# Attention state in 64-column chunks, the third token tile on the ACT queue, and a key fold interleaved with MLP units

## The chip, the cores and the metric

One core of one Trainium2 chip runs the whole kernel. The metric is the device time in microseconds of one execution (us), where lower is better. Engines are named as in the profile: PE multiplies matrices (PEld is its loading of weights, the stationary operand), DVE is the vector engine, ACT the scalar engine, POOL the general one, and SP only issues DMAs here.

## The reference

The input x has 2048 tokens of 640 features. It is normalised, and two branches read the normalised tokens: a linear attention with 32 heads of 20 columns, and a gated MLP with 1536 hidden columns. Their sum and x make the output.

```python
def _A_ref(x, wqkv, w_phi, wo):                      # S = 2048, D = 640, H = 32, Dh = 20
    q, k, v = split(x @ wqkv)                        # by head
    pq, pk = q @ w_phi, k @ w_phi                    # per head, 20x20
    phi_q = concat([softmax(pq), softmax(-pq)])      # 40 features per head
    phi_k = concat([softmax(pk), softmax(-pk)])
    kv, z = phi_k.T @ v, sum_s(phi_k)                # the state: 40 x 20 and 40 per head
    o = (phi_q @ kv) / (phi_q @ z + 1e-6)
    return merge_heads(o) @ wo
def _B_ref(x, w1, w3, w2):
    return (silu(x @ w1) * (x @ w3)) @ w2
xn = _layernorm(x)
out = x + _A_ref(xn, A_wqkv, A_w_phi, A_wo) + _B_ref(xn, B_w1, B_w3, B_w2)
```

## The kernel before

**How the work is tiled.** Tokens come in 16 tiles of 128, in `x_tok`, and in four blocks of 512 for the MLP. Features come in five chunks of 128. `xnT` holds the normalised tokens with features on partitions. Tiles 0 to 3 are transposed by PE (`xn_transpose`) and copied out of PSUM by ACT or DVE; the others by transposing DMAs on SP's queue. `w_phi` is folded into the key and query weights ahead of use: `fold_mm(1, dc)` makes chunk `dc` of `Wkp` with six small matmuls from `wqkT` (the key weights, loaded transposed by a DMA) and `BDc` (a block-diagonal `w_phi` made by POOL), and copies it out of PSUM. Values go to `v2` in 21 columns per head, of which the last is 1.0, so that the sum z comes with the same matmul.

**The attention state.** Key features lie in `ekt`. `kv_sum(half, k)` multiplies them with `v2` in 11 chunks of three heads (120 feature rows, 63 columns; the last chunk has two heads and 42 columns), each summed over the 16 token tiles. DVE multiplies the result with the mask `FM`, which keeps each head's own block, and writes it to `KVc`, a bf16 tile of 11 chunks of 63 columns that lie without a gap. `q_tok(t, k)` then takes one token tile: 11 matmuls with the transposed query features `EqT` as the stationary operand and one chunk of `KVc` as the moving operand, then a reciprocal and a product on DVE. `EqT` is written by a transposing DMA per token tile, from `eqt`, on SP's queue.

**What sets the order.** The program is written as twelve generator streams (`norms`, `transposes`, `fold_k`, `attention`, `mlps`, `outs` and others), each of which yields its next step or waits for a count in `done`. A planner holds a cost for every operation, takes at each step the stream whose head could start first by these costs, and appends its operations to the fixed instruction list of each engine. So an edit of one step can move others that it doesn't name. At run time each engine executes its list in order and waits on semaphores. All instructions are made by two helpers, so the profile names two lines: L102 (`op`) for computing and L114 (`dma`) for transfers.

**The opening.** `first_loads` (line 412) issues the first transfers. SP's queue has, in this order: token tile 0, chunks 0 and 1 of the value weights `wv`, token tile 2, chunks 2 and 3 of `wv`, chunk 4 of `wv`, token tile 3, a third of `w1` and of `w3` for the MLP, `w_phi`, the transposed key weights `wqkT`, and more tokens and weights. ACT's queue has token tile 1 alone. Each tile then goes through statistics (`ln_sums`, `ln_rstd`), `ln_apply` on DVE, `xn_transpose` on PE, copies to `xnT`, and the value matmuls `v_half` in two halves `q` of five matmuls each, which `v_out` copies to `v2`. `evac` gives a copy to ACT or DVE, whichever the planner believes free first. An MLP unit (`mlp(b, fc, k)`) has ten matmuls of 512 columns, one ACT operation and two on DVE; it needs all four tiles of its block.

**The key fold.** The stream `fold_k` (line 732) yields the five steps of `fold_mm(1, dc)` one after the other, with nothing that holds them apart:

```python
def fold_k():
    for dc in range(DC):
        yield lambda dc=dc: fold_mm(1, dc, banks(2))
    done["f"] += 1
```

The count `done["m"]` is that of the MLP units placed so far. `attention` goes on to the key features only once `done["f"]` is 1.

Of the kernel before, what the change touches and what calls it, by code (L numbers as in the profile page):

```python
# [3 lines left out]
ACT = mybir.ActivationFunctionType  # L4
ALU = mybir.AluOpType
# [5 lines left out]
H = 32  # L11
DH = 20
# [5 lines left out]
QC = 11  # L18
EPS = 1e-5
DEN_EPS = 1e-6  # L20
# [5 lines left out]
def heads_of_chunk(c):  # L26
    return (128 * c) // DH, (128 * c + 127) // DH
# [216 lines left out]
def bass_parallel_sum__linear_kernel_hedgehog__glu_gated_swiglu__prompt_kernel(  # L244
# [11 lines left out]
    bf = DT.bfloat16  # L256
# [6 lines left out]
    P = _Program(nc)  # L263
# [6 lines left out]
    def region(size):  # L270
        o = top[0]
        top[0] = o + (size + 31) // 32 * 32
        assert top[0] <= arena_size, top[0]
        return a0 + o

    def new(name, shape, dtype, offset=None):
        size = mybir.dt.size(dtype)
        for n in shape[1:]:
            size *= n
        return P.sbuf(name, shape, dtype, region(size) if offset is None else offset)  # L280
# [12 lines left out]
    FM = new("FM", [128, 6, 3], bf)  # L293
# [13 lines left out]
    x_tok = new("x_tok", [128, T, D], bf, RX)  # L307
# [22 lines left out]

    RW = region(13696)
    wqkT = new("wqkT", [128, 2 * DC, D], bf, RW)
    KVc = new("KVc", [128, QC, 63], bf, RW)
    eqt = new("eqt", [128, 3, QC * 128], bf, RW + 1408)
    o_tok = new("o_tok", [128, 3, D], bf, RW + 9856)
    EqT = [EqT0, EqT1]
# [5 lines left out]
    def bank(k, cols=512, off=0, rows=128):  # L342
        return PS[0:rows, k * 512 + off:k * 512 + off + cols]

    def bank2(k, cols):
        return PS[:, k * 512:(k + 2) * 512].rearrange("p (b c) -> p b c", c=512)[:, :, 0:cols]


    def mm(o, l, r, start, stop, shared=False, cost=None):
        n = free(r)  # L350
        P.op("PE", "matmul", [o], [l, r], (o, l, r),
             dict(start=start, stop=stop, skip_group_check=shared),
             cost=max(n / 2400 + 0.003, 0.055) if cost is None else cost)
# [5 lines left out]
    def free(ap):  # L359
        n = 1  # L360
        for s in ap.shape[1:]:
            n *= s
        return n
# [5 lines left out]
    def tt(eng, o, a, b, f, fast=1):  # L369
        c = 0.16 + free(o) / 960 / fast if eng == "DVE" else 0.2 + free(o) * 1.7 / 1000  # L370
        P.op(eng, "tensor_tensor", [o], [a, b], (o, a, b, f), cost=c)

    def stt(o, a, s, b, f0, f1):
        P.op("DVE", "scalar_tensor_tensor", [o], [a, b], (),
             dict(out=o, in0=a, scalar=s, in1=b, op0=f0, op1=f1), cost=0.16 + free(o) / 960)
# [7 lines left out]
    def evac(o, i):  # L383

        a = P.free["ACT"] + 0.17 + free(o) / 1200
        d = P.free["DVE"] + 0.14 + free(o) / 960 / (2 if i.dtype == bf else 1)
        copy("ACT" if a <= d else "DVE", o, i, 2 if i.dtype == bf else 1)
# [10 lines left out]
    x_t = A_x.rearrange("b (t p) d -> p (b t) d", p=128)  # L398
# [6 lines left out]
    def w13(a, b):  # L405
        P.dma("SP", w1_s[:, :, a:b], w1_t[:, :, a:b])
        P.dma("SP", w3_s[:, :, a:b], w3_t[:, :, a:b])

    def load_x(a, b):
        P.dma("SP", x_tok[:, a:b, :], x_t[:, a:b, :])  # L410

    def first_loads():
        load_x(0, 1)
        o = P.dma("ACT", x_tok[:, 1:2, :], x_t[:, 1:2, :])
        o.reads = P.regions(zero[:])
        for a, b in ((0, 2), (2, 4), (4, DC)):
            P.dma("SP", wv[:, a:b, :], wqkv_t[:, a:b, 2 * D:3 * D])
            if a != 2:
                load_x(2 + a // 4, 3 + a // 4)
        w13(0, 512)  # L420
        P.dma("SP", phi_s[:], phi_t)
        P.dma("SP", wqkT[:, DC:2 * DC, :], A_wqkv[:, D:2 * D], True)
        load_x(4, 8)
        load_x(8, 12)
        w13(512, 1024)
# [94 lines left out]
    def fold_mm(which, dc, k):  # L520
        first = [True, True]
        for e in range(DC):
            h0, h1 = heads_of_chunk(e)
            lo, hi = DH * h0, DH * (h1 + 1)
            for q in range(2):
                a, b = max(lo, 320 * q), min(hi, 320 * q + 320)
                if a < b:
                    mm(bank(k + q, b - a, a - 320 * q), wqkT[:, which * DC + e, 128 * dc:128 * dc + 128],
                       BDc[:, e, a - lo:b - lo], first[q], e == DC - 1 or (q == 0 and e == 2), True)
                    first[q] = False  # L530
        dst = (Wqp, Wkp)[which]
        evac(dst[:, dc, :].rearrange("p (b c) -> p b c", c=320), bank2(k, 320))
# [78 lines left out]
    def kv_sum(half, k):  # L611
        c0, c1 = ((0, 6), (6, QC))[half]
        for c in range(c0, c1):
            n = min(63, H * 21 - 63 * c)
            for t in range(T):
                m = min(128, (T - t) * 1280 - 120 * c)
                f = ekt[:].rearrange("p t f -> p (t f)")[:, 1280 * t + 120 * c:1280 * t + 120 * c + m]
                mm(bank(k, n, 63 * (c - c0))[0:m, :], f, v2[:, t, 63 * c:63 * c + n],
                   t == 0, t == T - 1, True, 0.03)
        n = min(6 * 63, H * 21 - 63 * c0)  # L620
        o = KVc[:, c0:c1, :].rearrange("p c (g d) -> p (c g) d", d=21)[:, 0:n // 21, :]
        i = bank(k, n).rearrange("p (g d) -> p g d", d=21)
        m = FM[:].rearrange("p c g -> p (c g)")[:, 0:n // 21]
        tt("DVE", o[:, :, 0:DH], i[:, :, 0:DH], m.unsqueeze(2).to_broadcast([128, n // 21, DH]), ALU.mult)
        stt(o[:, :, DH], i[:, :, DH], DEN_EPS / 2, m, ALU.add, ALU.mult)

    def q_tok(t, k):
        b, j = divmod(t, 4)
# [53 lines left out]
    def banks(n):  # L682

        def free_at(k):
            return max([o.end for i in range(k, k + n) for o in P.bank.get(("P", i), {}).values()],
                       default=0.0)
        return min(range(0, 8, n), key=free_at)

    done = dict.fromkeys(("w", "ln", "t", "f", "k", "v", "n", "kv", "p", "pn", "pt", "q", "o", "h", "m", "first"), 0)

    landed, pace, force = {}, [0], [False]

    def norms():
        yield lambda: (memset("DVE", zero[:], 0.0), memset("DVE", warm[:], 0.0), first_loads(), consts())
        yield lambda: act_sums(1)
        yield lambda: ln_stats(0, 1)
# [34 lines left out]

    def fold_k():
        for dc in range(DC):
            yield lambda dc=dc: fold_mm(1, dc, banks(2))
        done["f"] += 1

    done["w"] = 8
# [65 lines left out]
    def attention():  # L803
# [29 lines left out]
        while done["n"] < T:  # L833
            yield None
        yield lambda: kv_sum(0, banks(1))
        yield lambda: kv_sum(1, banks(1))
        done["kv"] = 1
        yield lambda: P.dma("SP", w2_s[:], B_w2.rearrange("(c p) d -> p c d", p=128))
# [23 lines left out]
    def outs():  # L862
        for t in range(T):
            while done["o"] <= t or done["h"] <= t // 4:
                yield None
            yield lambda t=t: out_tile(t, banks(2))

    streams = [norms(), transposes(), fold_k(), attention(), k_norms(), loads(), queries(), q_norms(),
               q_transposes(), o_transposes(), mlps(), outs()]
    MLPS, ATTN = 10, 3  # L870
    URGENT = {0: 4.0, 4: 4.0, 7: 4.0, 8: 4.0, 9: 4.0}
    n = len(streams)
    heads, alive = [None] * n, [True] * n
    while any(alive):
        best = None
        for i in range(n):
# [14 lines left out]
            if any(o.eng == "PE" for o in ops):  # L891
                at = max(P.ready(ops), P.free["PE"] + 0.15)
# [4 lines left out]
            else:  # L897
                at = P.start_of(ops[0])
                if i in URGENT:
                    now, mine = P.free["PE"], P.free[ops[0].eng]  # L900
                    if at <= max(now, mine) + 0.3 and at < now + URGENT[i]:
                        at = now + 0.1 - URGENT[i]
# [5 lines left out]
        i, ops, after = best[2:]  # L908
# [65 lines left out]
```

## Time and profile before

| | |
|---|---|
| median of 8 runs | 268.83 us (268.71 to 269.04) |
| the profiled execution's own time | 268.68 us |
| its span in the profile | 267.0 us |
| PE busy | 262.4 us, 98% of the span, 1951 matmuls |
| DVE, ACT, POOL busy | 182.8, 105.3, 96.2 us |
| granted PE clock | 1.00 |
| DMA traffic | 27.73 MB, mean 104 GB/s |

The span is what the profile covers; 1.7 us of the execution's time lie around it. Matmuls are pipelined: one of 63 columns is shown with 193 ns, but a new one can start every 30 ns or so. What a matmul costs the engine is therefore the distance between two starts, which the timeline gives as the distance of two groups divided by their count, and not its mean duration. A group named after its first shape can hold others: the ten matmuls of 63 columns and the one of 42 of a `q_tok` are shown as one group of eleven.

### The profile page before, as it was taken

To read this page: it belongs to the slowest core of one execution; us is meant where nothing else is said; L and a number is where in the kernel's file an instruction comes from. 1 tells how busy PE (TensorE), PEld (TensorE's weight loads), DVE (VectorE), ACT (ScalarE), POOL (GpSimd) and SP (SyncE) were. 2 spreads that over 40 slices of the span, in tenths; PEclk is the share of its full clock that TensorE was granted. 3 is DMA by queue.
4 is the path that set the end of the run, shared out by engine and by line. 5 is a ranking of instruction groups with operands and counts; after the bars stand their busy time and mean duration, and the time that the engine had idled before them with its cause. 6 is when DMAs were issued, how large, how long until landed. Compare 5 with 4: busy or idle time off the path is not lost.

```text
span 267.0 us, 4817 instructions
## 1 busy us (share of the span) xinstructions
PE 262.4 (98%) x1951; PEld 162.6 (61%) x1951; DVE 182.8 (68%) x315; ACT 105.3 (39%) x224; POOL 96.2 (36%) x107
## 2 busy tenths in 40 slices
PE   7999999999999999999999999999999999999996
PEld 2655666777645846567556565647455656777773
DVE  4669897998756697998697477758587955412112
ACT  5457978988565025440422404322244310000000
POOL 4313475799995163335233030340303330000000
PEclk9999999999999999999999999999999999999999
DMA  7993799620000198364643504260613035431211
GB/s 224 290 320 108 119 264 234 116 109 2 0 0 0 11 341 162 61 121 94 140 85 69 127 29 79 49 139 22 128 27 80 0 70 114 98 101 49 77 49 49
DMA packets 62742, 27.73 MB, mean 104 GB/s; under 512 B 49920, under 2 KB 62720, under 8 KB 62720
## 3 DMA queue, kind: packets, MB, share of 16 engines
q1 hardware_dynamic: 62576, 27.26, 42.8%
q8 instruction: 15, 0.25, 0.4%
q10 hardware_dynamic: 144, 0.16, 0.2%
q14 instruction: 7, 0.06, 0.1%
HBM read 12.81 MB, written 2.62 MB: 58 GB/s over the span
## 4 chain that ended last, share of the span: by engine, by line
PE 97%; DMA 1%; DVE 1%; ACT 0%; POOL 0%; issue 0%
PE PS L102 97%; DMA x_tok<-in_A_x_dram 1%; DVE bst L102 0%; ACT xnT L102 0%; POOL rstd L102 0%; DVE x_tok L102 0%; DVE xnT L102 0%; DVE xres L102 0%; DVE mv L102 0%
## 5 line engine op out<-in xcount | busy, mean ns | idle before, releaser
L102 PE MATMUL PS<-xnT,w_s 128*128 128x512 bf16 x480 | 107.7, 379 | 0.0
L102 PEld LDWEIGHTS PS<-xnT,w_s 128*128 128x128 bf16 x480 | 46.6, 98 | 52.1 <-ACT Wkp L102 0.2
L102 POOL TENSOR_TENSOR eqt<-eqt,rS 128x600 bf16<-128x600 bf16 (+1 forms) x32 | 41.1, 1307 | 92.5 <-DVE rS L102 92.5
L102 ACT ACTIVATE th<-PS 128x512 f32<-128x512 f32 x48 | 28.5, 597 | 80.8 <-PE PS L102 80.7
L102 PE MATMUL PS<-w_s,hT 128*128 128x320 bf16 (+2 forms) x384 | 54.9, 299 | 0.0
L102 DVE SCALAR_TENSOR_TENSOR t<-th,PS 128x512 bf16<-128x512 f32 x48 | 32.3, 673 | 27.3 <-ACT th L102 27.2
L102 PEld LDWEIGHTS PS<-w_s,hT 128*128 128x128 bf16 x384 | 37.1, 98 | 15.1
L102 POOL TENSOR_TENSOR ekt<-ekt,rS 128x640 bf16<-128x640 bf16 x32 | 39.5, 1274 | 6.7 <-DVE rS L102 6.7
L102 DVE TENSOR_TENSOR xres<-PS,xres 128x640 bf16<-128x640 f32 (+2 forms) x17 | 13.4, 786 | 37.7 <-PE PS L102 37.7
L102 ACT ACTIVATE eqt<-PS 128x240 bf16<-128x240 f32 (+1 forms) x96 | 27.1, 348 | 21.9 <-PE PS L102 17.9
L102 DVE SCALAR_TENSOR_TENSOR hT<-t,PS 128x512 bf16<-128x512 bf16 x48 | 33.0, 687 | 1.7
L102 DVE TENSOR_REDUCE S<-eqt 128x66 f32<-128x1320 bf16 x16 | 24.3, 1518 | 3.1 <-ACT eqt L102 3.1
L102 PE MATMUL PS<-wv,xnT 128*128 128x320 bf16 x160 | 24.5, 299 | 0.5 <-DVE xnT L102 0.2
L102 ACT ACTIVATE ekt<-PS 128x640 bf16<-128x640 f32 x32 | 22.4, 704 | 6.5 <-PE PS L102 5.9
L102 PE MATMUL PS<-wo_s,oT 128*128 128x320 bf16 (+2 forms) x160 | 24.5, 299 | 0.0
L102 PE MATMUL PS<-Wqp,xnT 128*128 128x360 bf16 (+1 forms) x160 | 24.2, 299 | 0.0
L102 PE MATMUL PS<-Wkp,xnT 128*128 128x320 bf16 x160 | 24.0, 299 | 0.0
L102 DVE TENSOR_REDUCE S<-ekt 128x64 f32<-128x1280 bf16 x16 | 23.0, 1437 | 0.0
L102 DVE RECIPROCAL rS<-S 128x64 f32<-128x64 f32 (+1 forms) x32 | 17.9, 560 | 3.3 <-POOL ekt L102 2.2
L102 PEld LDWEIGHTS PS<-Wqp,xnT 128*128 128x128 bf16 x160 | 15.2, 98 | 7.4
L102 PEld LDWEIGHTS PS<-wv,xnT 128*128 128x128 bf16 x160 | 15.3, 98 | 7.0 <-ACT xnT L102 0.7
L102 PEld LDWEIGHTS PS<-Wkp,xnT 128*128 128x128 bf16 x160 | 15.5, 98 | 6.2
(52 smaller groups left out, 152.8 us busy)
## 6 DMA issues: line engine op xcount, KB each, us to landing
w_s<-in_B_w_dram SPq DMA_DIRECT2D x6, 640.0 KB, 7.6
xres<-in_A_x_dram SPq DMA_DIRECT2D x16, 160.0 KB, 2.5
out_dram<-xres SPq DMA_DIRECT2D x15, 160.0 KB, 1.9
x_tok<-in_A_x_dram SPq DMA_DIRECT2D x3, 640.0 KB, 5.1
w_s<-in_B_w_dram SPq DMA_DIRECT2D x1, 1920.0 KB, 8.0
wo_s<-in_A_wo_dram SPq DMA_DIRECT2D x1, 800.0 KB, 4.7
wv<-in_A_wqkv_dram SPq DMA_DIRECT2D x2, 320.0 KB, 4.0
x_tok<-in_A_x_dram SPq DMA_DIRECT2D x3, 160.0 KB, 4.2
```

Source lines behind the costliest of these rows:

```text
L102: o = _Op(eng, lambda: m(*args, **kw), r, w, cost)
```

## The change

It has three parts. First, a chunk of `KVc` gets 64 columns in place of 63, with the last one unused, so that chunks begin 128 bytes apart; since heads are no longer evenly spaced over the whole tile, the masking in `kv_sum` works on four-dimensional views, and the second half, which ends with the chunk of two heads, is masked in two passes. Second, token tile 2 is issued by ACT's queue behind token tile 1, and SP's queue issues the three parts of `wv` one after the other and then token tile 3. Third, `fold_k` remembers the count of MLP units after its first step, and doesn't offer its third step before one more MLP unit is placed, and its fifth before two more are.

```diff
-    KVc = new("KVc", [128, QC, 63], bf, RW)
+    KVc = new("KVc", [128, QC, 64], bf, RW)
...
         o = P.dma("ACT", x_tok[:, 1:2, :], x_t[:, 1:2, :])
         o.reads = P.regions(zero[:])
+        P.dma("ACT", x_tok[:, 2:3, :], x_t[:, 2:3, :])
         for a, b in ((0, 2), (2, 4), (4, DC)):
             P.dma("SP", wv[:, a:b, :], wqkv_t[:, a:b, 2 * D:3 * D])
-            if a != 2:
-                load_x(2 + a // 4, 3 + a // 4)
+        load_x(3, 4)
...
-        n = min(6 * 63, H * 21 - 63 * c0)
-        o = KVc[:, c0:c1, :].rearrange("p c (g d) -> p (c g) d", d=21)[:, 0:n // 21, :]
-        i = bank(k, n).rearrange("p (g d) -> p g d", d=21)
-        m = FM[:].rearrange("p c g -> p (c g)")[:, 0:n // 21]
-        tt("DVE", o[:, :, 0:DH], i[:, :, 0:DH], m.unsqueeze(2).to_broadcast([128, n // 21, DH]), ALU.mult)
-        stt(o[:, :, DH], i[:, :, DH], DEN_EPS / 2, m, ALU.add, ALU.mult)
+        w = c1 - c0 - half
+        for a, b, g in ((0, w, 3), (w, c1 - c0, 2))[0:1 + half]:
+            o = KVc[:, c0 + a:c0 + b, 0:21 * g].rearrange("p c (g d) -> p c g d", d=21)
+            i = bank(k, 21 * g * (b - a), 63 * a).rearrange("p (c g d) -> p c g d", g=g, d=21)
+            m = FM[:, a:b, 0:g]
+            tt("DVE", o[:, :, :, 0:DH], i[:, :, :, 0:DH], m.unsqueeze(3).to_broadcast([128, b - a, g, DH]), ALU.mult)
+            stt(o[:, :, :, DH], i[:, :, :, DH], DEN_EPS / 2, m, ALU.add, ALU.mult)
...
     def fold_k():
         for dc in range(DC):
+            while dc and dc % 2 == 0 and done["m"] < at + dc // 2:
+                yield None
             yield lambda dc=dc: fold_mm(1, dc, banks(2))
+            if dc == 0:
+                at = done["m"]
         done["f"] += 1
```

In the instruction lists that come out, PE has the same 1951 matmuls in another order, from the third token tile on. The first difference, with the matmuls counted by shape:

```
before                                     after
 wv of tiles 0 and 1        320 x16         wv of tiles 0 and 1        320 x16
 transposes of tile 2       128 x5          transposes of tile 2       128 x5
 wv of tile 2, first half   320 x5          wv of tile 2, both halves  320 x10
 transposes of tile 3       128 x5          transposes of tile 3       128 x5
 wv: rest of tile 2, tile 3 320 x15         MLP unit                   512 x10
 two MLP units              512 x20         wv of tile 3               320 x10
 fold, five chunks          140/80 x30      fold, two chunks           140/80 x12
 MLP unit                   512 x10         MLP unit                   512 x10
 key features               320 x10         fold, two chunks           140/80 x12
 ...                                        two MLP units              512 x20
                                            fold, one chunk            140/80 x6
```

On DVE, the copy of tile 2's first value half now stands ahead of `ln_apply` of tile 3, and DVE copies chunks 0 and 1 of the transposed tiles 2 and 3 while ACT copies their chunks 2 to 4, behind value copies; before, DVE copied both parts of tiles 2 and 3. DVE gets one more pair of masking operations in `kv_sum`, and one of the five `Wkp` copies that ACT had. The later order of MLP units, query tiles and output tiles is changed throughout, and with it the order of transfers on SP's queue: one `EqT` transpose now stands ahead of the load of `w2`.

## The prediction
> **What bounds the kernel now.** I read the page first: its first part and the chain of work that ended last.
>
> ```profile
> PE 262.4 (98%) x1951; PEld 162.6 (61%) x1951; DVE 182.8 (68%) x315; ACT 105.3 (39%) x224; POOL 96.2 (36%) x107
> ...
> PE 97%; DMA 1%; DVE 1%; ACT 0%; POOL 0%; issue 0%
> ```
>
> PE is the bound, and by so much that any time it loses anywhere is added to the end, and any matmul that gets shorter is taken from it. So two things decide: where PE stands still, and the distance between its matmuls. The busy times by stretch (length, then PE, PEld, DVE and so on) say where it stands still:
>
> ```profile
> 5.49:10.23 4.74, 4.25 (x36) 2.79 (x36) 4.00 (x13) 2.87 (x7) 1.67 (x3) 1.00 1.06 339
> 10.23:13.24 3.01, 3.01 (x26) 2.15 (x27) 1.60 (x5) 0.88 (x2) 1.17 (x3) 1.00 1.34 220
> ...
> 19.42:92.00 72.58, 72.58 (x627) 47.84 (x628) 59.74 (x100) 53.02 (x91) 49.09 (x54) 1.00 0.40 91
> ...
> 104.00:230.00 126.00, 126.00 (x890) 74.92 (x888) 93.65 (x158) 39.25 (x108) 33.37 (x26) 1.00 0.38 80
> ```
>
> After 19.42 PE never waits. Before that, the timeline shows the stretches that the change rearranges (start, length, group):
>
> ```profile
> 9.57 0.44 PE L102 MATMUL PS<-ident,x_tok 128*128 128x128 bf16 x5
> 10.23 0.85 PE L102 MATMUL PS<-wv,xnT 128*128 128x320 bf16 x5 [0.22 <-DVE xnT L102]
> 10.92 0.44 PE L102 MATMUL PS<-ident,x_tok 128*128 128x128 bf16 x5
> 11.20 2.20 PE L102 MATMUL PS<-wv,xnT 128*128 128x320 bf16 x15
> ...
> 17.55 1.86 PE L102 MATMUL PS<-BDc,wqkT 128*128 128x140 bf16 x30
> ...
> 9.77 0.44 ACT L102 ACTIVATE v<-PS 128x320 bf16<-128x320 f32 x1 [0.24 <-PE PS L102]
> ...
> 9.88 0.56 DVE L102 COPY xnT<-PS 128x256 bf16<-128x256 bf16 x2 [0.49 <-PE PS L102]
> 10.35 0.44 DVE L102 TENSOR_SCALAR x_tok<-x_tok,mv,rstd 128x640 bf16<-128x640 bf16 x1
> ...
> 12.76 0.49 DVE L102 CAST v<-PS 128x320 bf16<-128x320 f32 x1 [0.97 <-PE PS L102]
> ```
>
> Tile 2 is transposed at 9.57, its copy lets the value matmuls start at 10.23 (a stall of 0.38 against the usual distance of 0.056 after a transpose), and from there PE has no gap up to the fold. Tile 3 was normalised by DVE from 10.35, in time for 10.92, and its copies are covered by five value matmuls of tile 2.
>
> **The key fold.** Matmuls of 140 columns start 61 ns apart, those of 80 columns 35 ns: thirty need 20 x 61 + 10 x 35 = 1.57 us. The fold takes 19.42 - 17.55 = 1.87. The 0.30 is two waits, 0.11 inside it and 0.17 ahead of the next MLP unit, both for copies out of PSUM. With MLP units of ten matmuls at 216 ns, 2.16 us, between the pairs of chunks, a copy of about 0.71 us (ACT's mean for `Wkp`) has cover. The copy that goes to DVE has no row; scaled from the 0.49 us of half its columns it is under 1 us, and the 2.16 us cover it too. Worth: -0.28.
>
> **The opening in its new order.** Up to 9.57 the lists of PE, DVE and ACT are as before. Then, by the rows above:
> - Value matmuls of tile 2 start at 10.23 again. The third needs chunks 2 to 4, now ACT's copy. ACT is in its value copy until 9.77 + 0.44 = 10.21; the same copy took 0.49 when ACT did it for tile 0; so it ends at about 10.68 and PE goes on at 10.73 (a copy's end to PE's start is 0.05 throughout). At 136 ns a matmul the third was due at 10.50: stall 0.22.
> - Ten matmuls instead of five follow, so PE is free at 10.73 + 8 x 0.136 = 11.82. But `ln_apply` of tile 3 now stands on DVE behind the copy of tile 2's first value half, which waits for the fifth matmul (start 11.00, done 0.30 later): 11.32, plus 0.49 of copy, plus 0.44 of `ln_apply`, makes 12.25, and tile 3's transposes start at 12.30. Stall 0.48. Behind that DVE copy nothing else was due; PE itself is what waits.
> - The next work is an MLP unit that needs tile 3 itself, no longer matmuls of tile 2. Two transposes (second result at 12.30 + 0.06 + 0.22 = 12.58), a copy of 0.29 and 0.05 give 12.93, where PE was free at 12.58: stall 0.35. Its third matmul is due at 13.36, and ACT's copy of chunks 2 to 4 ends about 13.28.
>
> Sum of new stalls 1.05. Bounds: 0.8, if ACT and DVE overlap starts as their back-to-back copies do (up to 0.08 each), and 1.3, if each handover costs 0.05 more.
>
> The fold then starts at 12.93 + 2.16 + 1.36 = 16.45 instead of 17.55. Its `wqkT` landed at 16.25, and it needs `BDc`, done at 14.04: both in time, the first by 0.2 alone. Its issue leaves 0.47 earlier (below), so I add nothing; if it landed later, each 0.1 costs 0.1.
>
> **The third tile on ACT's queue.** ACT's first issue takes 0.38 from 1.03; a second moves its table load from 1.43 to 1.8 and the end of the warming operation from 2.94 to 3.3. ACT next waits for tile 1, at 3.50: hidden, with 0.2 to spare. SP's later issues leave 0.43 to 0.53 earlier, each from the row of one issue. No landing there was waited for: tile 2 landed at 5.88, DVE took it at 5.90 having finished the work before it at 5.85; `wv` landed at 4.75, 6.75 and 7.15 against uses at 6.25, 7.40 and about 7.9. So at most 0.05 is gained, and a loss needs tile 1 (3.47) or the first part of `wv` to land later than they are used; the latter may slip by 160 KB, some 0.5 us at the 320 GB/s of the page's row, and has 1.5. Worth 0. From the Trainium skill, "DMA: Bandwidth & Descriptors", section "Issuing engines are not separate DMA queues", comes a rule against this part: a second issuing engine saves only the issuing sequencer's time, since all transfers share the same DMA engines. By it the part is worth at most its 0.47 us of issue, and nothing where transfers bound the opening.
>
> **The 64-column chunks.** The timeline gives the price now (a whole `q_tok` and the group after it; then `kv_sum` and the group after it):
>
> ```profile
> 104.11 0.50 PE L102 MATMUL PS<-KVc,EqT 128*128 128x63 bf16 x11
> 104.46 0.77 PE L102 MATMUL PS<-Wqp,xnT 128*128 128x360 bf16 x4
> ...
> 86.86 5.27 PE L102 MATMUL PS<-v,ekt 128*128 128x63 bf16 x176
> 91.97 1.89 PE L102 MATMUL PS<-xnT,w_s 128*128 128x512 bf16 x8
> ```
>
> A `q_tok` takes 0.35 for 11 matmuls, 31.8 ns each; `kv_sum` takes 5.11 for 176, 29.0 each. Taken one at a time, the starts in a `q_tok` show a pattern that is the same in all 16: 28 ns after chunk 0, 34 after chunk 1, 32 after chunks 2 to 7, 28 after chunk 8, 32 after chunk 9, 29 after the short chunk. Chunks 0 and 8 are the only ones that begin at a multiple of 16 bytes (0 and 8 x 126 = 1008). With 128-byte chunks all begin as chunk 0 does: 10 x 28 + 29 = 309 ns instead of 343, times 16 is -0.54. Bounds: -0.61 if the short chunk falls to the 25 it has in `kv_sum`; above, no gain at all, or +0.4 if every chunk went like chunk 1. Against it speaks `kv_sum`, whose moving operand `v2` starts at the same odd offsets at 28 to 30 ns mostly; so the offset alone may not be the cause. By its 29.0 the gain would be 16 x (343 - 11 x 29) = -0.38. I take -0.52, near the rows of chunks 0 and 8, as these are the same instruction on the same tile. The Trainium skill, "TensorE: Matmul & The Clock Gate", section "Back-to-back issue gap", knows no alignment: N/2.4 + 2.5 ns, 28.75 for 63 columns; and 25 for the short chunk as its floor; by it, as an estimate, this part would be near -0.49, with the 32 ns now seen unexplained.
>
> The masking gets one more product and one more small operation on DVE, under 0.5 us by the rows of 0.39 and 0.22 for the old second half. The first `q_tok` follows an MLP unit and a query tile later, some 3.5 us: hidden.
>
> **The rest of the order.** From 19.42 on the same matmuls come in another sequence, and the only new waits I can find, adding the rows' durations along the new lists, are of `q_tok` for `EqT`: a transposing DMA behind another one and 3.6 to 4.0 us from issue to landing. The tightest, near 175, lands as it is needed. Before has such a place too, near 193, where it cost the weight load 0.20 of idle time and the matmuls nothing. From 0 to 0.4; I take 0.05. No gain is possible here, as PE had no gap to lose.
>
> **Sum.** -0.28 + 1.05 + 0 - 0.52 + 0.05 = +0.30. Against the profiled execution's 268.68 that is 268.98; the median of the eight runs is 0.15 above that execution, so 269.1. A change of 0.2% is 0.54 us, about what a measurement can tell here; +0.30 is within it.
>
> **The rivals.**
> - *Alignment buys nothing* (slower): the `q_tok` matmuls stay near 31.8 ns because something other than the chunk's address sets them. Then +0.82, 269.65. It decides from a gain under 0.28, a mean above 29.6 ns. For it: `kv_sum`'s odd offsets. Against: chunk 8 is fast in all 16 blocks.
> - *A late transpose* (slower): the new order puts `EqT` behind other SP transfers, and two or three `q_tok` wait 0.2 to 0.4 each, 0.4 to 1.2 in place of the 0.05: +0.65 to +1.45, 269.5 to 270.3. Against: no such gap in before, whose spare was as small.
> - *The opening gets nearer to DVE's speed* (faster): the three new stalls come out at half, 0.5, since ACT's and DVE's copies start on parts I count as done, and the short chunk gains too: -0.28 + 0.5 - 0.61 = -0.39, 268.44; beyond -0.54 only if the stalls are under 0.35. The instruction lists speak against it: the waits are between engines, in a chain of five handovers.
> - *The change doesn't do what it says*: the tile begins 32 bytes past a multiple of 128, so chunks are 128 apart but not on multiples. Chunk 0 lies so now and is fast: same number as the forecast.
>
> **How the numbers follow.** Forecast and its variants within their bounds 0.57 (own range 268.7 to 269.5, of which a sixth lies past +0.54); alignment nothing 0.17, nearly all slower; late transposes 0.14; faster 0.12, of which two thirds go past -0.54. Slower: 0.10 + 0.16 + 0.14 = 0.40; faster 0.08; same 0.52. The range leaves out the outer halves of the late transposes and of the faster case and the slowest of the first rival, 0.16 together: 268.4 to 269.8.
>
> **What would show it.** In the profile after: `q_tok` groups of 0.31 from start to next group (right) or 0.35 (wrong); a DVE value copy at about 11.3 followed by `ln_apply`, with PE waiting 0.4 to 0.5 for `x_tok`; the first MLP unit near 12.9; the fold's waits gone; PE without gaps from 13 on. It is wrong if PE has a gap after 20, if the first transposes no longer start at 5.49, or if `wqkT` lands after the fold is due.

## The result and the profile after

The changed kernel takes 269.86 us (median of 10 runs, 269.54 to 270.05), the kernel before 268.81 in the same comparison: a ratio of 1.0038, 95% interval 1.003 to 1.0046. So it is slower, by 1.05 us, where +0.30 was predicted. The profiled execution took 270.05, with a span of 268.3; against 268.68 and 267.0 before, that is a span longer by 1.3. The median of the ten runs lies 0.19 below this execution.

First the page of the kernel after, its busy times and the shares of the chain that ended last:

```profile
PE 262.4 (98%) x1951; PEld 162.0 (60%) x1951; DVE 183.3 (68%) x316; ACT 106.5 (40%) x225; POOL 96.2 (36%) x107
...
PE 92%; DMA 4%; DVE 2%; POOL 1%; ACT 1%; issue 0%; ACTq 0%
```

PE's busy time, matmuls and clock are what they were. Its share of the chain fell from 97% to 92%, and DMA's rose from 1 to 4: the end is now set at some places by something that PE waits for. The timeline of the opening shows the first of these places (start, length, group, idle time and who ended it):

```profile
6.60 0.49 DVE L102 BATCH_NORM_STATS2 bst<-x_tok 128x6 f32<-128x320 bf16 x1 [0.66 <-DMA x_tok<-in_A_x_dram]
...
7.50 0.45 PE L102 MATMUL PS<-ident,x_tok 128*128 128x128 bf16 x5
...
10.62 1.67 PE L102 MATMUL PS<-wv,xnT 128*128 128x320 bf16 x10 [0.22 <-DVE xnT L102]
...
11.65 0.49 DVE L102 CAST v<-PS 128x320 bf16<-128x320 f32 x1 [1.09 <-PE PS L102]
12.06 0.61 DVE L102 TENSOR_SCALAR x_tok<-x_tok,mv,rstd 128x640 bf16<-128x640 bf16 x1
...
12.73 0.45 PE L102 MATMUL PS<-ident,x_tok 128*128 128x128 bf16 x5 [0.43 <-DVE x_tok L102]
...
13.40 0.82 PE L102 MATMUL PS<-xnT,w_s 128*128 128x512 bf16 x3 [0.22 <-DVE xnT L102]
```

The idle times in brackets count from a matmul's shown end. The gaps of PE given below count from when the next matmul could have started by the usual distance, and so are up to 0.2 longer: tile 3's transposes start 0.73 after the last value matmul, where 0.14 is usual, a gap of 0.60.

This is the chain that the prediction wrote down: DVE copies tile 2's first value half at 11.65, then normalises tile 3, and PE waits for that, and once more for tile 3's copies ahead of the first MLP unit. It comes 0.4 later than predicted, because the first transposes start at 5.59 instead of 5.49 and tile 1's at 7.50 instead of 7.12: DVE waited for tile 2 until 6.58, which before had landed at 5.88.

The second place is late. Pieces of the chain of work that ended last (start, length, what):

```profile
13.40 179.19 PE PS L102 x1349
...
196.58 2.48 POOL eqt L102 x2
199.06 4.65 DMA EqT<-eqt
...
203.76 62.25 PE PS L102 x468
```

PE runs from 13.40 without a gap, then waits at 203.3 for an `EqT` transpose and starts the query tile at 203.76, 0.46 after its work had ended. That gap was not there before. The fold's two waits are gone (timeline, PE):

```profile
16.93 0.79 PE L102 MATMUL PS<-BDc,wqkT 128*128 128x140 bf16 x12
17.56 2.32 PE L102 MATMUL PS<-xnT,w_s 128*128 128x512 bf16 x10
19.72 0.79 PE L102 MATMUL PS<-BDc,wqkT 128*128 128x140 bf16 x12
20.35 3.40 PE L102 MATMUL PS<-xnT,w_s 128*128 128x512 bf16 x15
```

12 fold matmuls take 17.56 - 16.93 = 0.63, which is 8 x 61 + 4 x 35 ns with nothing added. And a query tile takes 0.32 instead of 0.35:

```profile
98.87 0.47 PE L102 MATMUL PS<-KVc,EqT 128*128 128x63 bf16 x11
99.19 7.07 PE L102 MATMUL PS<-xnT,w_s 128*128 128x512 bf16 x32
```

Over all 16 of them, the starts lie 5.13 us apart in sum, against 5.49 before. The profiled executions' difference of 1.3 is thus accounted for, by PE's gaps in us:

| | predicted | measured |
|---|---|---|
| first transposes (tile 0 landed 0.11 later) | 0 | +0.10 |
| tile 1's transposes (tile 2 landed 0.70 later) | 0 | +0.28 |
| third value matmul of tile 2 | +0.22 | +0.13 |
| tile 3's transposes behind DVE's value copy | +0.48 | +0.60 |
| MLP unit behind tile 3's copies | +0.35 | +0.38 |
| the fold's two waits | -0.28 | -0.28 |
| query tiles in 64-column chunks | -0.52 | -0.36 |
| waits for `EqT` | +0.05 | +0.46 |
| sum | +0.30 | +1.31 |

### The profile page after: what moved, and what is told of

The parts are those of the page before. It is cut to its first block, busy times and chain, and to the rows that moved or that the text cites. A ratio compares the mean times of both kernels' runs of the same rounds, so it can differ in the third digit from the quotient of the medians.

```text
span 268.3 us, 4820 instructions
## 1 busy us (share of the span) xinstructions
PE 262.4 (98%) x1951; PEld 162.0 (60%) x1951; DVE 183.3 (68%) x316; ACT 106.5 (40%) x225; POOL 96.2 (36%) x107
## 4 chain that ended last, share of the span: by engine, by line
PE 92%; DMA 4%; DVE 2%; POOL 1%; ACT 1%; issue 0%; ACTq 0%
PE PS L102 92%; DMA x_tok<-in_A_x_dram 2%; DMA EqT<-eqt 2%; POOL eqt L102 1%; ACT eqt L102 1%; DVE S L102 1%; DVE x_tok L102 0%; DVE xnT L102 0%; DVE rS L102 0%; DVE v L102 0%; DVE bst L102 0%; ACTq L114 0%; DVE xres L102 0%; DVE zero L102 0%; DVE warm L102 0%
## 5 line engine op out<-in xcount | busy, mean ns | idle before, releaser
L102 PEld LDWEIGHTS PS<-wo_s,oT 128*128 128x128 bf16 x160 | 15.2, 98 | 6.3
```

The lines of the kernel that those rows point to most:

```text
L102: o = _Op(eng, lambda: m(*args, **kw), r, w, cost)
```

## The experiments

For all but one of them the planner's run was recorded: the stream taken at each step, and at each choice the engine of a copy or the bank of PSUM. The kernel then replays these two lists instead of planning, so that one edit moves nothing else. In `STEPS` a letter is a stream (a `norms`, b `transposes`, c `fold_k`, d `attention`, i the `EqT` transposes, k `mlps`, l `outs`); in `CHOICES` A and D are ACT and DVE, a digit is a bank. Each time stands against the kernel before, 268.76 to 268.77 in these comparisons.

### The chunks alone

The order of before, replayed, with the first part of the change:

```diff
-    KVc = new("KVc", [128, QC, 63], bf, RW)
+    KVc = new("KVc", [128, QC, 64], bf, RW)
 ...                                        (and the masking by four-dimensional views)
+STEPS = ( steps of the kernel before )
```

> Only the 64-column chunks, with the steps and copy choices of the kernel before held fixed. Theory (the address of a chunk sets the distance of its matmul): the 176 matmuls of the query tiles take 5.13 us instead of 5.49, as in the profile after, so 268.81 - 0.36 = 268.45 us (268.3 to 268.6), and nothing else moves. Rival (the gain is eaten, by the extra masking pass or by waits that appear elsewhere): 268.7 to 268.9.

Measured: 268.37 us (268.18 to 268.58), ratio 0.9981 (0.9968 to 0.9994). The part is worth 0.39 by itself (the interval allows 0.16 to 0.86); the 63-column matmuls start 29.0 to 29.2 ns apart in every tile, the short one takes 29.

### The ACT queue alone

```diff
+        P.dma("ACT", x_tok[:, 2:3, :], x_t[:, 2:3, :])
         for a, b in ((0, 2), (2, 4), (4, DC)):
             P.dma("SP", wv[:, a:b, :], wqkv_t[:, a:b, 2 * D:3 * D])
-            if a != 2:
-                load_x(2 + a // 4, 3 + a // 4)
+        load_x(3, 4)
+STEPS = ( steps of the kernel before )
```

> Only token tile 2 on ACT's queue (and SP's queue without it), with the steps and copy choices of the kernel before held fixed. Theory (on its own queue the tile shares the DMA engines with the value weights and lands later, near 6.6 us instead of 5.9; DVE, which works in order, holds ln_apply of tile 1 behind it): PE starts tile 1's transposes near 7.5 instead of 7.1, and the time is 268.81 + 0.3 to 0.4 = 269.1 to 269.2 us. Rival (the prediction's, the landing was never waited for): 268.8 us.

Measured: 268.85 (268.76 to 269.09), ratio 1.0005 (0.9996 to 1.0013): no effect that can be told from none.

### The changed kernel with tile 2 back on SP's queue

The lines of the last diff the other way round, on the steps of the kernel after.

> The changed kernel with its steps and copy choices held fixed, but token tile 2 back on SP's queue between the parts of the value weights. Theory: tile 2 lands near 5.9, tile 1's transposes start near 7.1, and the time is 269.86 - 0.3 to 0.4 = 269.45 to 269.55 us; the three later stalls of the opening (0.13, 0.60, 0.38) stay. Rival (the late landing is absorbed by those stalls): 269.8 us.

Measured: 269.84 (269.67 to 269.93), ratio 1.004 (1.0026 to 1.0054), the changed kernel's own time. Tile 2 landed at 6.49 on SP's queue too, and the wait ahead of tile 1's transposes stayed. So the theory that ACT's queue brings tile 2 later, formed from the one trace after, fell. In the profiled executions of all kernels here tile 2 landed at 5.13 to 6.49 when SP issued it and at 5.20 to 6.58 when ACT did. By the Trainium skill, "DMA: Bandwidth & Descriptors", section "Issuing engines are not separate DMA queues", a second issuing engine saves no more than issue time. Both runs agree with it, and here even that time was worth nothing.

### DVE's value copy given to ACT

```diff
 CHOICES (on the steps of the kernel after)
-"0A1A2A3DAA4A5A6D7A2D3A0D1A4..."
+"0A1A2A3DAA4A5A6D7A2A3A0D1A4..."
```

> The changed kernel with its steps held fixed, but the copy of tile 2's first value half goes to ACT instead of DVE. Theory (ln_apply of tile 3 is late only since it stands behind that copy on DVE): PE's stall of 0.60 ahead of tile 3's transposes falls to 0.1 or less, and the time is 269.86 - 0.4 to 0.55 = 269.3 to 269.45 us. Rival (the stall moves on: ACT's copy of tile 3's chunks 2 to 4 is then late by its own value copies): the MLP unit waits instead and the time is 269.6 to 269.8 us.

Measured: 269.31 (269.04 to 269.47), ratio 1.0018 (1.001 to 1.0027): 0.55 of the 1.05 is given back by one letter. The timeline shows how:

```profile
10.34 0.44 DVE L102 TENSOR_SCALAR x_tok<-x_tok,mv,rstd 128x640 bf16<-128x640 bf16 x1
...
11.51 0.44 ACT L102 ACTIVATE v<-PS 128x320 bf16<-128x320 f32 x1 [0.67 <-PE PS L102]
...
11.98 0.44 PE L102 MATMUL PS<-ident,x_tok 128*128 128x128 bf16 x5
```

DVE normalises tile 3 at 10.34 instead of 12.06, and PE goes from the value matmuls to the transposes without waiting. ACT had been idle for 0.67 before its copy: the choice of DVE cost PE time while ACT stood by.

### The transpose ahead of the store

```diff
 STEPS (on the steps of the kernel after)
-"...jkkdghlikigjkhdl..."
+"...jkkdghilkigjkhdl..."
```

> The changed kernel with its steps recorded and replayed, and one pair of steps exchanged: the EqT transpose that the query tile near 203.3 waits for is issued on SP's queue ahead of the store of an output tile instead of behind it. Its source eqt is finished by POOL at 192.9, but SP, which issues in order, stands at the store until DVE has added the residual, at 198.64, and so issues the transpose at 199.06. Theory (a transpose held up behind a store): it leaves near 193, lands before 198, PE's wait of 0.46 ahead of that query tile is gone, and the time falls from 269.86 to about 269.4. Rival (transposes are slow as such, or PE waits next for the second transpose, which comes 1.4 later): the wait stays or moves on by one query tile, 269.8.

Measured: 269.21 (268.86 to 269.43), ratio 1.0013 (1.0005 to 1.0022). PE has no gap after 12.70. SP's queue in the kernel after, then in this one:

```profile
198.68 0.34 SPq L114 DMA_DIRECT2D out_dram<-xres  x1
199.06 3.96 SPq L114 DMA_TRANSPOSE EqT<-eqt  x2
```

```profile
192.19 1.38 SPq L114 DMA_TRANSPOSE EqT<-eqt  x1
...
197.97 0.34 SPq L114 DMA_DIRECT2D out_dram<-xres  x1
198.47 1.39 SPq L114 DMA_TRANSPOSE EqT<-eqt  x1
```

The transpose that the query tile needs leaves at 192.19, 10.4 us before PE comes to it at 202.60, and lands at 195.73; in the kernel after it left 4.2 us before PE came. The chain of the kernel after had put POOL's `eqt` ahead of it, which ends near 199.1, just as the store has been issued; that POOL work belongs to the second of the two transposes. What the first one waited for was the store in front of it in SP's order. The gain is 0.65, where the gap in the profile was 0.46; the difference of 0.19 is not located. The two medians' intervals, some 0.2 us to either side of each, leave room for it.

### The fold alone

The planner writes the order here, with only the third part of the change in its streams.

```diff
         for dc in range(DC):
+            while dc and dc % 2 == 0 and done["m"] < at + dc // 2:
+                yield None
             yield lambda dc=dc: fold_mm(1, dc, banks(2))
+            if dc == 0:
+                at = done["m"]
```

> The kernel before with the third part of the change alone (the key fold waits for MLP units after its first two and next two chunks); the planner chooses the rest of the order again. Theory (the MLP units are only placed at a price): the fold's two waits, 0.28, go, but in the order that the planner then writes the copies of Wkp come late for PE near 23, a wait that adds up to 1.3 by the rows of the copies: about 269.8. Rival (the part is worth what the prediction's sum gave it, whatever stands around it): -0.28, 268.5.

Measured: 270.03 (269.94 to 270.1), ratio 1.0045 (1.0033 to 1.0058). The timeline of PE and ACT:

```profile
22.24 1.73 ACT L102 ACTIVATE x_tok<-x_tok,rstd 128x640 bf16<-128x640 bf16 x2
...
22.51 0.79 PE L102 MATMUL PS<-BDc,wqkT 128*128 128x140 bf16 x12
...
23.88 0.68 ACT L102 ACTIVATE Wkp<-PS 128x640 bf16<-128x640 f32 x1
...
24.62 0.49 PE L102 MATMUL PS<-BDc,wqkT 128*128 128x140 bf16 x6 [1.31 <-ACT Wkp L102]
```

The second pair of chunks is done, and ACT has two normalisations of 0.87 in front of the copy that PE needs. PE stands still for 1.47; the two old waits of 0.28 are gone. Their difference of 1.19 is nearly the 1.27 by which the kernel is slower. The order of ACT's list, not the length of its copy, sets the price.

### All waits taken away

The steps of the kernel after, with the last two edits and a third: the second value half of tile 2 (a `d` step) comes behind tile 3's transposes.

```diff
 STEPS
-"adaaaaaaaaabbdbbaaaddddbbdadbabkddcc..."    "...kkdghlikig..."
+"adaaaaaaaaabbdbbaaaddddbbdababdkddcc..."    "...kkdghilkig..."
```

> The changed kernel with its steps recorded and replayed, and three edits of the order: ACT makes the copy of tile 2's first value half, so that DVE goes to ln_apply of tile 3 at once; the second value half of tile 2 comes behind tile 3's transposes, so that PE has work while their copies are made; and the EqT transpose near 199 is issued ahead of the output tile's store. Theory (the time lost is the sum of these three waits, and nothing else): 269.86 - 0.55 - 0.38 - 0.46 = 268.5 or a little less, 0.1 above the kernel before's order with 64-column chunks (268.37), from the wait for the third value matmul of tile 2. Rival (waits that are taken away come back further on, at the fold, which would start near 15.4, or at another transpose): 268.9 or more.

Measured: 268.25 (268.0 to 268.33), ratio 0.9977 (0.9968 to 0.9986). From 10.82 on PE has no gap: the waits did not come back elsewhere. The fold starts at 15.72, and `wqkT` had landed at 14.26. The time is 0.2 below the theory's sum; with the 0.65 that the exchange of store and transpose gave, in place of 0.46, that sum is 268.28.

A fourth edit gives back to DVE the copy of tile 2's chunks 2 to 4:

```diff
-"0A1A2A3DAA4A5A6D7A2A0D..."
+"0A1A2A3DAA4A5A6D7D2A0D..."
```

> The kernel without the three waits (268.25), with a fourth edit of the order: DVE instead of ACT copies chunks 2 to 4 of the transposed tile 2, as in the kernel before. Theory (the wait of 0.13 ahead of the third value matmul of tile 2 is ACT's value copy in front of that copy): the wait goes and nothing takes its place, 268.1. Rival (the time goes to the next wait: the fold, reached 0.13 earlier, waits for wqkT, which landed between 14.3 and 14.9 in the runs so far, against a need near 15.4): 268.25.

Measured: 268.16 (268.0 to 268.3), ratio 0.9976 (0.9967 to 0.9985). A piece of the chain that ended last, in which PE works from tile 2's values to its last matmul without a wait:

```profile
10.31 253.77 PE PS L102 x1901
```

The wait of 0.13 is gone from the trace; the median falls by 0.09, and the two kernels' runs overlap. This version, with the change's 64-column chunks, spread fold and later order, is the fastest here and beats the kernel before by 0.6 us.

### What makes a packed chunk slow

Three kernels on the steps of before, each run once, ask why packed chunks take 32 ns. Their times are 268.62, 274.13 and 274.26 us; the last two pay for extra copies ahead of the query tiles, see the end. The first gives each chunk its own offset:

```diff
-    KVc = new("KVc", [128, QC, 63], bf, RW)
+    KVc = new("KVc", [128, QC, 80], bf, RX + 18688)
-                ... KVc[:, c, 0:n],
+                ... KVc[:, c, SHIFT[c]:SHIFT[c] + n],
+SHIFT = (0, 1, 2, 4, 8, 16, 0, 3, 6, 12, 0)
```

> The kernel before with its steps recorded and replayed, and the chunks of KVc 160 bytes apart, each shifted by a number of elements, so that chunks 0 to 10 begin 0, 2, 4, 8, 16, 0, 0, 6, 12, 24 and 0 bytes past a multiple of 32; the masking is done chunk by chunk, on DVE. Read is the distance from each chunk's matmul to the next one's, averaged over the 16 query tiles; 63 columns each, and 42 for chunk 10. Theory (a moving operand that doesn't begin at a multiple of 16 bytes costs 3 to 6 ns more): chunks 0, 4, 5, 6 and 9 take 28 to 29 ns, chunks 1, 2, 3, 7 and 8 take 31 to 34. Rival (the gap between chunks or the pad column is what counts, not the address): all ten take 28 to 29.

Measured, in ns from chunk 0 to 9: 28, 29, 29, 34, 28, 28, 29, 29, 34, 28. Chunks 1, 2 and 7 begin off a multiple of 16 and are fast, and so is chunk 9, whose 24 is no multiple of 16 either, though the expectation counted it as one; chunks 3 and 8 are slow. Neither theory holds. The second gives all chunks of one tile the same offset:

```diff
+    def shifted(t):                              (called one tile ahead)
+        for a, z, w in ((0, 10, 63), (10, QC, 42)):
+            copy("DVE", KVs[t % 2][:, a:z, t:t + w], KVc[:, a:z, 0:w])
-                ... KVc[:, c, 0:n],
+                ... KVs[t % 2][:, c, t:t + n],
```

> The kernel before with its steps recorded and replayed; KVc stays packed and masked as it was, but each query tile t multiplies with a copy of it (made by DVE, one tile ahead) whose chunks lie 160 bytes apart and all begin 2t bytes past a multiple of 32, t = 0 to 15. Read is the mean distance between the 63-column matmuls of each tile. In the kernel with a different offset for each chunk, offsets of 8 and 12 took 34 ns and offsets 0, 2, 4, 6, 16 and 24 took 28 to 30. Theory (the offset of the chunk by itself sets the distance): tiles 4 and 6 take 33 to 34 throughout, tiles 0 to 3, 8 and 12 take 28 to 30. Rival (a matmul is slowed by what lies before it, such as a neighbour in the same line or a run of unaligned chunks): tiles 4 and 6 are no slower than tiles 1 to 3 and 12.

Mean distances after chunks 1 to 9 of a tile: 29.6 and 29.9 for tiles 4 and 6, 29.6, 29.8 and 29.6 for tiles 2, 3 and 12, all others from 2 on 29.2 to 30.0 (tiles 0 and 1 don't count, since PE ran at half its clock there, see the end). So offset 8, 34 ns in the kernel before this one, is 29.6 here: the theory fell, and the offset of a chunk by itself is not the cause. The third changes the distance between chunks:

```diff
+    def spaced(t):
+        return KVs[t % 2][:].rearrange("p c d -> p (c d)")[:, 0:QC * STEP[t]].rearrange("p (c d) -> p c d", d=STEP[t])
-                ... KVc[:, c, 0:n],
+                ... spaced(t)[:, c, 0:n],
+STEP = (80, 63, 64, 65, 66, 67, 68, 70, 72, 63, 64, 71, 76, 65, 63, 64)
```

> As the kernel with one offset for each query tile, but the chunks of the copies begin at a multiple of 32 bytes only in the first one, and lie a number of columns apart that changes from tile to tile: 80, 63, 64, 65, 66, 67, 68, 70, 72, 63, 64, 71, 76, 65, 63, 64 for tiles 0 to 15. So tiles 1, 9 and 14 have the packed chunks of the kernel before, in another place, and the others a gap of 2 to 34 bytes. Read is the mean distance of the 63-column matmuls of each tile. Theory (a chunk that begins right where the last one ended costs 2 ns more, whatever the offsets): tiles 1, 9 and 14 take 31 to 32, all others 29 to 30. Rival (the copies lie in another part of the memory, and that made them faster): tiles 1, 9 and 14 take 29 to 30 too.

| columns from chunk to chunk | 63 | 64 | 65 | 66 | 67 | 68 to 80 |
|---|---|---|---|---|---|---|
| mean ns after chunks 1 to 9 | 31.9, 31.6 | 29.2, 29.1, 29.1 | 30.8, 30.6 | 30.3 | 30.0 | 29.1 to 29.4 |

(Tile 1 doesn't count, as above.) Packed chunks are slow in this place too, so the rival fell. The theory holds in the main: packing costs 2.6 ns against a step of 64. But with 2 to 4 columns of gap, 0.9 to 1.7 of them remain, and 64 columns are as good as 80. That the step between chunks alone decides is not shown. In the first of the three kernels chunks 3 and 8 took 34 ns with at least 19 columns of gap on either side. And in `kv_sum` of the kernel before, where the moving operands of one chunk lie 672 columns apart, every third or fourth matmul of chunks 1 to 6 and 9 takes 31 to 34 ns, while none of chunks 0, 7 and 8 takes more than 30. What is shown is that a whole tile of packed chunks runs at 31.6 to 31.9, and one with a step of 64, or of 68 to 80, at 29.1 to 30.0. Why stays open.

## Why the prediction was wrong

**Right.** That the opening loses more than the fold gains, by the three waits named, in their places and nearly in their sizes: +1.05 predicted, +1.11 in the profile (+0.94 with the 0.43 that tile 3's wait has in two other kernels with this opening, the ones with tile 2 back on SP's queue and with the transpose ahead of the store). Giving DVE's copy to ACT returned 0.55 for a step priced at 0.48. The fold's -0.28 came as written, in this order. The queue is worth nothing, and `wqkT`, `BDc` and the landing of `wv` cost nothing.

**The step that failed most: "The rest of the order", taken as 0.05.** The prediction used 3.6 to 4.0 us from issue to landing for a transpose and called the place near 175 the tightest. The one that waits is near 203: behind a store that holds SP until DVE has added the residual, and 4.65 us long. At 4.0 it would have landed at 203.06, before PE needed it at 203.3, so the wait took both: the late issue, without which it is gone (the transpose ahead of the store), and a transfer longer than the rows that the prediction went by. A gap after 20 was one of its own signs of being wrong. The three profiled kernels that keep this order show the gap: 0.46, 0.59 and 0.46. The late-transpose rival named the mechanism ("behind other SP transfers"), gave it 0.14 and expected two or three waits; it was one, and its 0.46 lies a little above the 0.2 to 0.4 given for each.

**The second: "The 64-column chunks", taken as -0.52.** A nearer row stood beside it. `kv_sum`'s 29.0 ns gave -0.38, and the prediction took the 28 of chunks 0 and 8 instead. (That 29.0 has the short chunks of 25 in it; the 63-column matmuls of `kv_sum` lie 29.4 apart.) The 28 are the distances of single matmuls among slower ones; a series at the fast pace settles at 29.1, with only the first at 28 to 29. Measured are -0.36 in the profile and -0.39 between medians. The short chunk stayed at 29. The reason given, a start at a multiple of 16 bytes, fell with the number: chunks that begin 2, 4 or 6 bytes past one took 29 in the first of the three kernels, and chunks with one offset in common 29.2 to 30.0, whatever it was. So the gain came, but not for that reason. The Trainium skill, "TensorE: Matmul & The Clock Gate", section "Back-to-back issue gap", gives a formula for an isolated matmul that makes 28.75 ns for 63 columns, close to the 29.1 that spaced chunks take. The 31.8 of packed ones lie above it, and the short chunk's 29 above the 25 that the prediction took from there.

With these two terms as measured the sum is 0.41 + 0.16 higher: 269.67, inside the range. The rest, 0.19, stays open. It is as much as the transpose ahead of the store gave beyond the gap of 0.46, so the wait for `EqT` may be longer in the median than in the profiled run. Or it belongs to the opening. In the profiled run the opening lost 0.44 more than the sum has there: 0.10 and 0.28 by landings that scatter from run to run on either queue, and 0.12 at tile 3, where `ln_apply` took 0.61 instead of 0.44 in this execution alone; the smaller differences are -0.09 and +0.03. But that run is itself 0.19 slower than the median.

**A gap in the reasoning that the number doesn't show.** The prediction costed the fold's new waits at nothing because MLP units of 2.16 us cover a copy of 0.71. The fold alone shows that this is no cover if ACT's list has other work ahead of the copy: 1.47 of wait in another order.

## What to carry to other kernels

When the bound engine has no slack, an edit that frees it in one place and lets a planner reorder the rest is judged by the new order, not by its intention: here the chunks were worth -0.39, the fold's waits -0.28 and the queue nothing, and the order cost 1.7; four edits of it by hand turned +1.05 into -0.6. On an engine that issues in order, look for the entry that waits for a result (a store) in front of one that could leave (a transpose). And where a matmul is short, price a change of layout by a long series of the same shape, not by the single fastest ones.

## What the runs showed of the hardware that was not expected

**Transposes in flight while a program packet was fetched landed late.** While the late transpose was on its way, the transfers in the kernel after look so (40 slices of 198 to 205 us, busy tenths; then the queue of instruction packets: packets, MB, share of the 16 engines):

```profile
DMA  0000000019970899999990000039999999999999
...
q8 instruction: 1, 0.02, 1.0%
```

The transposes stop at about 201.7 for 0.9 us and go on. The trace has the one packet, 16 KB, from 200.82 for 1.10 us. The same is seen in five other kernels with such a packet at 200 to 202: the transposes then in flight took 4.46 to 5.26 us, while those after 110 without any packet took 3.5 to 4.0 in all kernels. A packet near 126, where a transpose had just been issued, went with 3.6 to 4.1, and packets that came 3.3 us or more after the issue with 3.6 to 3.9. The store just ahead is not what makes them late: five other transposes of the kernel after leave 0.4 us behind a store too, and take 3.61 to 3.73. And the transpose near 147 took 4.1 to 4.2 in the five kernels of this order in which an 8 KB packet was fetched during it, but 3.56 in the one with tile 2 back on SP's queue, where that packet came at 151.19, after the landing at 150.82. That the packet is the cause is argued from these coincidences; it wasn't tried.

**After 3.6 us of waiting PE ran at half its rate for about as long.** In the kernel with one offset per tile, PE waited for DVE's extra copies ahead of the first query tile. The windows (length, then PE, PEld, DVE, ACT, POOL busy, the granted clock, DMA share, GB/s):

```profile
104.00:108.00 4.00, 0.43 (x6) 0.13 (x5) 2.45 (x5) 1.45 (x6) 0.28 (x1) 0.97 0.42 80
108.00:111.00 3.00, 3.00 (x21) 1.89 (x21) 2.97 (x4) 0.80 (x2) 2.41 (x2) 0.50 0.00 0
```

At the clock of 0.50 the 63-column matmuls start 53 ns apart. The trace grants 0.50 from 107.77 for 3.41 us. In the kernel with one step per tile the same wait was followed by 3.41 us at 0.50 too, from 109.27, which is 1.3 after PE had gone on. The fold's wait of 1.47 in the other kernel had no such sequel. So a bound engine that is made to wait this long pays twice: here 3.6 us of waiting, and about 1.6 us lost to half speed.
